# Three buffers for v and for raw weight words, with a new order of loads and new ranks, in a fused attention and mixture-of-experts kernel

## The chip, the cores and the metric

The kernel runs on one core of a Trainium2 chip. The metric is the device time of one execution in microseconds (us), the median of several runs. The engines are TensorE (PE for matmuls, PEld for its weight loads), VectorE (DVE), ScalarE (ACT), GpSimd (POOL) and SyncE (SP), which only issues DMA transfers.

## What is computed

Three layers follow each other. The first is Nyström attention over 4 batches, 8 heads, 576 tokens and 64 dimensions with 32 landmarks a head:

```python
A = sm(q, k_lm); Bm = sm(q_lm, k_lm); C = sm(q_lm, k)
Z = Bm.transpose(0, 1, 3, 2) / (norm1(Bm) * norminf(Bm) + 1e-06)
for _ in range(6):
    Z = 2 * Z - Z @ Bm @ Z
x = A @ Z @ C @ v
```

The second is a gated layer on the 2304 tokens of width 512: `h = x @ w_in` (512 x 2048), `g = h * clip(h + 3, 0, 6) / 6`, `x = g @ w_out` (2048 x 512). The third routes each token to one of 8 experts by `argmax(x @ w_gate)`, applies `relu(x @ w1) @ w2` of that expert up to a capacity, and scales by the token's gate probability. The weights w_in and w_out arrive as 64-bit words and have to be turned into 32-bit floats on the chip.

## The kernel before

The work falls into four stretches. In the first, q, k and v are loaded for 8 units (4 batches x 2 groups of 4 heads) and the attention of each unit is worked out: `turn_qk` forms landmark sums (on PE by `fold` matmuls into `ps_f`, L537, for units 0 to 3; on DVE by `sums`, L550, and one matmul, L554, for units 4 to 7), `landmark_scores` and `token_scores` form the scores (`pb`), `gather_v` multiplies the softmax with v (`ps_ct` L696, `ps_cl` L704, `pw` L715), `norms` (`ps_m` L670) and `newton` (`pn` L735, `px` L759) make the inverse. `project` multiplies the result with w_in (`ps_v` L362 into `vv`). In the second stretch `first` (`ph`, 6 matmuls each, L389) and `second` (`py`, 12 matmuls each, L433) run the gated layer for four quarters of the 2048 columns (`fq`) and 6 blocks of 288 tokens; `lasts` does the same for the last two blocks. The third stretch is the expert layer, unit by unit (`run_unit`: L1094, L1132, L1163, L1170). At the end a flag `redo` decides by a branch (`tc.If`, L1364) whether a general and slow path has to run over again; with these inputs it does not.

The order of the instructions in the first two stretches is made by a list scheduler in Python, the class `Order` (L39 to L107). Each job is a generator that yields steps (engine, estimated cost, buffers to take, events to wait for). `run` takes the step that can start first by its estimates, and among steps that can start at about the same time the one with the lowest rank; ranks come from the table `RANK`. `LOADS` is the order in which the loads of q and k (`qk`), v (`v`), w_in (`in`) and w_out (`out`) are issued; the loads of this list follow each other in that order on SP (`issue`). `BLOCKS` is the order of the blocks within each quarter. Each engine then runs its own instructions strictly in the order written, and waits for semaphores where a producer is late.

While the first `ph` has not been placed (`state["cold"]`), the scheduler puts filler matmuls on PE into the idle time that it expects: `keep_warm`, L983, one per 0.115 us beyond the first 0.3 us; they are the `warm` matmuls of L984 and compute nothing that is used.

Two buffer counts matter here. `convert` (L243) loads a 128 x 512 piece of 64-bit words into a tile `raw` (512 KB, L254), which is free again when ACT, DVE and, for the first quarter's pieces, POOL have made floats of it. `load_v` (L509) loads a unit's v into `vm` and `vl` (L515, L516), which are free again after the unit's `pw` matmuls. Both have two buffers, and the scheduler's table of slots has `raw=2` and `v=2`. The loads of the first expert's w1 (`w1_first`, L919) use `raw` too.

Of the kernel before, what the change touches and what calls it, by code (L numbers as in the profile page):

```python
# [8 lines left out]
F32 = mybir.dt.float32  # L9
# [3 lines left out]
U32 = mybir.dt.uint32  # L13
# [3 lines left out]
ET = mybir.EngineType  # L17
# [93 lines left out]

LOADS = [('qk', 1), ('in', 2), ('in', 1), ('qk', 0), ('v', 0), ('v', 1), ('in', 0), ('in', 3), ('qk', 2), ('v', 2), ('qk', 3), ('out', 1), ('out', 0), ('out', 2), ('qk', 4), ('v', 3), ('v', 4), ('out', 3), ('qk', 5), ('v', 5), ('qk', 7), ('v', 6), ('in', 6), ('in', 7), ('qk', 6), ('v', 7), ('in', 5), ('in', 4)]

RANK = {'w': -298.73, 'evict': 81.41, 'late': -13.54, 'fill': -244.58, 'logit': 110.18, 'route': -102.73, 'ahead': 67.77, 'unit2': 113.59, 'unit': 84.25, 'first2': 135.87, 'second2': 135.87, 'V2': -23.09, 'W': -6.44, 'u0': -30.37, 'u1': 44.61, 'u2': 38.52, 'u3': 45.53, 'u4': 84.73, 'u5': 65.31, 'u6': 98.5, 'u7': 118.66, 'cin0': 197.19, 'cin1': -0.9, 'cin2': 305.36, 'cin3': -23.6, 'cin4': 88.15, 'cin5': 450.88, 'cin6': 188.03, 'cin7': 280.69, 'cout0': -18.86, 'cout1': -66.49, 'cout2': 34.96, 'cout3': 65.88, 'V0': -74.78, 'V1': 84.97, 'V3': 134.52, 'V4': -441.95, 'V5': 37.92, 'V6': -57.56, 'V7': 31.31, 'out_1': 232.01, 'in_1': -9.42, 'wg_1': 188.44, 'out_2': 226.5, 'in_2': -334.43, 'wg_2': 114.87, 'out_3': -0.02, 'in_3': -179.05, 'wg_3': -27.51, 'C0': -161.31, 'C1': -15.08, 'C2': 6.94, 'C3': 1.79, 'C4': -17.7, 'C5': 55.68, 'C6': 42.33, 'C7': -71.74, 'A0': 130.29, 'A1': 103.73, 'A2': 144.67, 'A3': 116.13, 'A4': 122.48, 'A5': 121.43, 'A6': 133.45, 'A7': 202.82, 'B0': 44.41, 'B1': 144.53, 'B2': 64.17, 'B3': 62.65, 'B4': 51.27, 'B5': 35.89, 'B6': 91.91, 'B7': -6.21, 'Cv0': 42.94, 'Cv1': 52.0, 'Cv2': 35.34, 'Cv3': -62.91, 'Cv4': 45.36, 'Cv5': 17.68, 'Cv6': 36.1, 'Cv7': 38.02, 'Z0': -12.13, 'Z1': -62.3, 'Z2': -52.99, 'Z3': -37.97, 'Z4': -19.17, 'Z5': -52.94, 'Z6': -166.92, 'Z7': 12.86, 'sum0': 92.52, 'sum1': -22.5, 'sum2': 12.35, 'sum3': 52.44, 'sum4': 36.8, 'sum5': 57.28, 'sum6': -84.97, 'sum7': 33.35}

BY_PE = (0, 1, 2, 3)
BLOCKS = ((0, 0), (0, 1), (0, 2), (0, 3), (0, 4), (0, 5), (1, 0), (1, 3), (1, 2), (1, 1), (1, 4), (1, 5), (2, 0), (2, 2), (2, 3), (2, 5), (2, 1), (2, 4), (3, 2), (3, 0), (3, 1), (3, 3), (3, 4), (3, 5))
ROUTED = (0, 1, 3)  # L120
COMPACT = (2, 3, 4, 5, 6, 7)
G_BUFS, R_BUFS, QT_BUFS = 8, 2, 6


@with_exitstack
def nystrom_moe_kernel(ctx, tc, qt, kt, v, w_in, w_out, w_gate, w1, w2, capacity, out, dims, dbg=None):
    nc = tc.nc
    B, H, S, D = dims
    NT, DM = out.shape
    DFF = w_in.shape[1]  # L130
    E, _, F2 = w1.shape
# [3 lines left out]
    P = 128  # L135
# [3 lines left out]
    QW = DFF // NQ  # L139
# [880 lines left out]
    with tc.tile_pool(name="units", bufs=1, reuse_waits="tile") as up, \  # L1020
# [160 lines left out]
        def run_unit(i):  # L1181
# [11 lines left out]
            for t in range(NST):  # L1193
# [251 lines left out]
```

## Time and profile before

| what | value |
|---|---|
| median of 3 runs | 534.06 us (533.92 to 536.21) |
| the profiled execution's own time | 534.44 us |
| its span, first to last instruction | 532.7 us |
| PE busy | 518.9 us, 97% of the span |
| PEld busy | 452.3 us, 85% |
| DVE, ACT, POOL busy | 349.3, 293.9, 192.9 us (66%, 55%, 36%) |
| HBM read, written | 45.89 MB, 12.98 MB |

The profile shows one execution. The engines run beside each other, so their busy times overlap; PE is busy nearly all the time, though what it does in the first 50 us includes the filler matmuls, which count as busy. The time of an execution is a little more than its span (534.44 beside 532.7). The granted clock (PEclk) is the share of full speed that TensorE was allowed.

### The profile page before, as it was taken

How to read it: one execution, taken by the hardware profiler on the slowest of the kernel's cores; microseconds unless marked ns; L12 is line 12 of the kernel's file. 1: busy time of each engine (PE TensorE's matmuls, PEld its weight loads, DVE VectorE, ACT ScalarE, POOL GpSimd, SP SyncE). 2: the span in 40 equal slices, each digit the busy share in tenths (PEclk: the TensorE clock that was granted, in tenths of full speed). 3: DMA queues.
4: the chain of work that ended last, by engine and by line, in shares of the span. 5: the costliest groups of instructions: out<-in, count | busy, mean ns of one | idle time of the engine just before them, and what ended most of it. 6: DMA issues, size and time to landing. Idle time of an engine off the chain costs nothing. (4 is left out here: it accounts for less than half of the span.)

```text
span 532.7 us, 12062 instructions
## 1 busy us (share of the span) xinstructions
PE 518.9 (97%) x4781; PEld 452.3 (85%) x4781; DVE 349.3 (66%) x788; ACT 293.9 (55%) x684; POOL 192.9 (36%) x247
## 2 busy tenths in 40 slices
PE   8997999999999999999999999999999999999996
PEld 6664787968889998999998899998897899689784
DVE  1779867766479986675945555467735958987700
ACT  3776775966668554554545443444446564864411
POOL 3357967878434333311522112222160070016000
PEclk9999989999999999999999999999999999999999
DMA  7946741112352541214200020128921470510011
GB/s 292 312 178 222 270 151 49 38 46 75 89 184 93 189 143 51 76 40 135 80 1 1 1 90 2 41 93 281 323 96 41 172 281 0 175 53 23 2 50 44
DMA packets 24242, 59.74 MB, mean 112 GB/s; under 512 B 2928, under 2 KB 7536, under 8 KB 24176
## 3 DMA queue, kind: packets, MB, share of 16 engines
q1 hardware_dynamic: 23360, 58.60, 32.3%
q8 instruction: 39, 0.64, 0.5%
q10 hardware_dynamic: 816, 0.28, 0.2%
q14 instruction: 27, 0.22, 0.1%
HBM read 45.89 MB, written 12.98 MB: 111 GB/s over the span
## 5 line engine op out<-in xcount | busy, mean ns | idle before, releaser
L433 PE MATMUL py<-ghi,wo 128*128 128x288 f32 x768 | 159.1, 299 | 0.4 <-DVE yacc L445 0.4
L433 PEld LDWEIGHTS py<-ghi,wo 128*128 128x128 f32 x768 | 124.0, 190 | 5.1 <-issue 2.1
L389 PE MATMUL ph<-at,vv 128*128 128x288 f32 x768 | 120.8, 300 | 0.9 <-DVE st L662 0.8
L419 POOL TENSOR_TENSOR glo<-r,ghi 128x288 fp32r<-128x288 f32 x81 | 66.5, 830 | 150.4 <-ACT ghi L412 123.9
L433 PE MATMUL py<-glo,wo 128*128 128x288 f32 x384 | 113.9, 297 | 0.0
L389 PEld LDWEIGHTS ph<-at,vv 128*128 128x128 f32 x768 | 106.6, 188 | 8.6 <-issue 4.8
L400 ACT ACTIVATE r<-ph,half 128x288 f32<-128x288 f32 x128 | 63.6, 500 | 64.3 <-PE ph L389 54.2
L402 DVE SCALAR_TENSOR_TENSOR r<-r,ph 128x288 f32<-128x288 f32 x128 | 56.1, 447 | 29.0 <-ACT r L400 28.2
L433 PEld LDWEIGHTS py<-glo,wo 128*128 128x128 f32 x384 | 72.7, 189 | 0.0
L1163 PE MATMUL ps_o<-w2s,hT 128*128 128x512 f32 x288 | 66.2, 390 | 0.0
L1163 PEld LDWEIGHTS ps_o<-w2s,hT 128*128 128x128 f32 x288 | 53.8, 188 | 13.6 <-issue 2.4
L1053 POOL TENSOR_TENSOR w2s<-wi,w2s 128x512 fp32r<-128x512 f32 x24 | 31.5, 1353 | 88.1 <-ACT w2s L1052 88.1
L445 DVE TENSOR_TENSOR yacc<-py,yacc 128x288 f32<-128x288 f32 x72 | 32.5, 452 | 42.3 <-PE py L433 42.1
L412 ACT ACTIVATE ghi<-r 128x288 fp32r<-128x288 f32 x96 | 41.1, 441 | 23.1 <-DVE r L402 20.4
L1140 DVE TENSOR_TENSOR mix<-ps,mix 128x288 f32<-128x288 f32 x56 | 23.9, 451 | 11.6 <-PE ps L1132 11.0
L276 POOL TENSOR_TENSOR wo<-cvt,wo 128x512 fp32r<-128x512 f32 x16 | 21.9, 1368 | 22.7 <-ACT wo L274 22.6
L369 DVE TENSOR_TENSOR vv<-ps_v,vv 128x512 fp32r<-128x512 f32 x32 | 21.4, 683 | 11.4 <-ACT vv L367 11.3
L1079 ACT ACTIVATE hT<-mix 128x288 fp32r<-128x288 f32 x32 | 13.7, 443 | 26.8 <-DVE mix L1140 26.8
L735 PEld LDWEIGHTS pn<-yy 128*128 128x128 f32 x112 | 16.8, 189 | 9.4 <-issue 3.9
L735 PE MATMUL pn<-yy 128*128 128x96 f32 (+2 forms) x112 | 22.3, 294 | 0.8 <-POOL yy L687 0.5
L367 ACT ACTIVATE vv<-ps_v 128x512 fp32r<-128x512 f32 x32 | 18.2, 597 | 6.5 <-PE ps_v L362 6.3
L1174 ACT ACTIVATE rows_o<-ps_o,prob 128x512 f32<-128x512 f32 x12 | 8.3, 688 | 24.2 <-PE ps_o L1163 19.4
(219 smaller groups left out, 840.5 us busy)
## 6 DMA issues: line engine op xcount, KB each, us to landing
raw<-in_moe_w_in SPq DMA_DIRECT2D x16, 512.0 KB, 3.9
raw<-in_moe_w_out SPq DMA_DIRECT2D x16, 512.0 KB, 3.9
wi<-in_moe_w SPq DMA_DIRECT2D x6, 1024.0 KB, 6.6
r_d<-r SPq DMA_DIRECT2D x32, 144.0 KB, 1.8
vm<-in_v SPq DMA_DIRECT2D x8, 512.0 KB, 5.8
raw<-in_moe_w SPq DMA_DIRECT2D x4, 1024.0 KB, 5.9
qT<-in_q SPq DMA_DIRECT2D x6, 576.0 KB, 6.6
qT<-in_k SPq DMA_DIRECT2D x6, 576.0 KB, 7.7
```

What stands on the lines that cost most here:

```text
L276: nc.gpsimd.tensor_tensor(dst[1], xf, dst[0].bitcast(F32), op=ALU.subtract)
L389: nc.tensor.matmul(ph, lhsT=vv[pair][g][a][:, b, f * P:(f + 1) * P], rhs=at[pair][c][:, g, tok], start=n == 0, stop=n == 3 * NG - 1)
L400: nc.scalar.activation(r, ph, AF.Relu, bias=half, scale=1.0 / 6.0)
L402: nc.vector.scalar_tensor_tensor(r, r, 1.0, ph, op0=ALU.min, op1=ALU.mult)
L412: nc.scalar.activation(ghi, r, AF.Copy)
L419: nc.gpsimd.tensor_tensor(glo, r, ghi.bitcast(F32), op=ALU.subtract)
L433: nc.tensor.matmul(py, lhsT=w[a][:, f, d * P:(d + 1) * P], rhs=gh[f][c], start=f == 0 and n == 0, stop=f == NF - 1 and n == 2)
L445: nc.vector.tensor_tensor(y, py, y, op=ALU.add)
L735: nc.tensor.matmul(pn[:, cols], lhsT=yy[:, 0:P], rhs=yy[:, cols], start=True, stop=True)
L1053: engine.tensor_tensor(dst[1], src, dst[0].bitcast(F32), op=ALU.subtract)
L1140: plus = lambda dst, ps, x: nc.vector.tensor_tensor(dst, ps, x, op=ALU.add)
L1163: nc.tensor.matmul(ps, lhsT=hT[a][:, f, cols], rhs=w2s[c][:, f, :], start=n == 0, stop=n == 3 * FC - 1)
```

## The change

The tiles `vm`, `vl` and `raw` get three buffers, in the tile pools and in the scheduler's table of slots. `LOADS`, `BLOCKS` and nearly all numbers of `RANK` are replaced, so that the scheduler writes another order on every engine. A hint for the branch at the program's end is added for SP and ACT, and the scratch for dynamic DMA, which only the general path uses, is halved. From L1199 on, line numbers of the changed kernel are one higher.

```diff
-LOADS = [('qk', 1), ('in', 2), ('in', 1), ('qk', 0), ('v', 0), ('v', 1), ('in', 0), ('in', 3), ('qk', 2), ('v', 2), ('qk', 3), ('out', 1), ('out', 0), ('out', 2), ('qk', 4), ('v', 3), ('v', 4), ('out', 3), ('qk', 5), ('v', 5), ('qk', 7), ('v', 6), ('in', 6), ('in', 7), ('qk', 6), ('v', 7), ('in', 5), ('in', 4)]
+LOADS = [('qk', 1), ('qk', 0), ('in', 2), ('v', 0), ('in', 1), ('v', 1), ('in', 0), ('in', 3), ('qk', 2), ('v', 2), ('qk', 3), ('out', 0), ('v', 4), ('qk', 4), ('out', 3), ('out', 2), ('out', 1), ('v', 3), ('qk', 5), ('v', 7), ('in', 7), ('in', 6), ('v', 5), ('qk', 7), ('qk', 6), ('in', 4), ('in', 5), ('v', 6)]
...
-G_BUFS, R_BUFS, QT_BUFS = 8, 2, 6
+G_BUFS, R_BUFS, QT_BUFS, V_BUFS, RAW_BUFS = 8, 2, 6, 3, 3
...
-        raw = stage.tile([P, QW, 2], U32, tag="raw", name="raw")
+        raw = stage.tile([P, QW, 2], U32, tag="raw", name="raw", bufs=RAW_BUFS)
...
-    order = Order(dict(s=3, b=2, h=2, y=1, r3=2 * NF, g=2 * NF, r=R_BUFS, raw=2, cvt=2, part=1, qT=QT_BUFS, sums=2, lm=2,
-                       a1=2, a2=1, ec=2, eb=4, yy=4, rx=4, xx=2, ct=1, v=2))
+    order = Order(dict(s=3, b=2, h=2, y=1, r3=2 * NF, g=2 * NF, r=R_BUFS, raw=RAW_BUFS, cvt=2, part=1, qT=QT_BUFS, sums=2, lm=2,
+                       a1=2, a2=1, ec=2, eb=4, yy=4, rx=4, xx=2, ct=1, v=V_BUFS))
...
-        vm = late.tile([P, 4, 4 * D], F32, tag="vm", name="vm")
+        vm = late.tile([P, 4, 4 * D], F32, tag="vm", name="vm", bufs=V_BUFS)
...
-        c["vl"] = vl = late.tile([D, 4, D], F32, tag="vl", name="vl")
+        c["vl"] = vl = late.tile([D, 4, D], F32, tag="vl", name="vl", bufs=V_BUFS)
...
-        raw = stage.tile([P, F2], F32, tag="raw", name="raw_e")
+        raw = stage.tile([P, F2], F32, tag="raw", name="raw_e", bufs=RAW_BUFS)
...
+                    tc.mark_branch_hint_location("again", engines=(ET.SP, ET.Activation))
...
-            nest.enter_context(tc.If(again > 0))
+            nest.enter_context(tc.If(again > 0, label="again"))
...
-    nc = bacc.Bacc("TRN2", target_bir_lowering=False, num_devices=1, dynamic_dma_scratch_size=4096)
+    nc = bacc.Bacc("TRN2", target_bir_lowering=False, num_devices=1, dynamic_dma_scratch_size=2048)
```

How the order moves, at three places. First SP, the start of the program; `yacc_129` and `yacc_130` take q and k of unit 1, `yacc_127` and `yacc_128` those of unit 0 (a piece of the difference):

```order
+L1442 BRANCH_PREFETCH_HINT
 L506 DMA yacc_129<-in_q 128x1152
 L506 DMA yacc_130<-in_k 128x1152
-L254 DMA raw<-in_moe_w_in 128x1024 x2
 L506 DMA yacc_127<-in_q 128x1152
 L506 DMA yacc_128<-in_k 128x1152
-L515 DMA vm<-in_v 128x1024
-L516 DMA vl<-in_v 64x256
+L254 DMA raw<-in_moe_w_in 128x1024
+L515 DMA vm<-in_v 128x1024
+L516 DMA vl<-in_v 64x256
+L254 DMA raw<-in_moe_w_in 128x1024
```

Unit 0's q and k now stand right behind unit 1's; two pieces of w_in that stood ahead of them follow, with a v between them. The branch hint stands at the very start.

Second SP, from the loads of unit 3 to those of unit 4, with buffer numbers; before (`qT_432` and `qT_436` belong to unit 3, `qT_678` and `qT_683` to unit 4):

```order
L506 DMA qT_432<-in_q 128x1152
L506 DMA qT_436<-in_k 128x1152
L254 DMA raw_492<-in_moe_w_out 128x1024
L254 DMA raw_521<-in_moe_w_out 128x1024
L254 DMA raw_674<-in_moe_w_out 128x1024
L506 DMA qT_678<-in_q 128x1152
L506 DMA qT_683<-in_k 128x1152
L515 DMA vm_689<-in_v 128x1024
L516 DMA vl_690<-in_v 64x256
```

And now (`qT_417` and `qT_422` unit 3, `qT_486` and `qT_494` unit 4):

```order
L506 DMA qT_417<-in_q 128x1152
L506 DMA qT_422<-in_k 128x1152
L254 DMA raw_457<-in_moe_w_out 128x1024
L515 DMA vm_468<-in_v 128x1024
L516 DMA vl_469<-in_v 64x256
L506 DMA qT_486<-in_q 128x1152
L506 DMA qT_494<-in_k 128x1152
L254 DMA raw_521<-in_moe_w_out 128x1024
L254 DMA raw_584<-in_moe_w_out 128x1024
L254 DMA raw_671<-in_moe_w_out 128x1024
```

One piece of w_out instead of three stands ahead of unit 4's q and k; the other three have moved behind them.

Third PE, the stretch that leads to the first `ph`; before:

```order
L984 MATMUL warm<-ident 128x256
L578 MATMUL pb<-qT,lm 32x288 x8
L715 MATMUL pw<-vm,ct 32x64 x16
L715 MATMUL pw<-vl,ctl 32x64 x4
L670 MATMUL ps_m<-eb,mask_73 128x64
L696 MATMUL ps_ct<-ident,ec 128x128 x4
L735 MATMUL pn<-yy 128x96
L389 MATMUL ph<-at_117,vv_123 128x288
```

And now, where two fillers and the two rows of `pw` (L715) lie between the last row shown and the first `ph`:

```order
L984 MATMUL warm<-ident 128x256
L554 MATMUL ps_f<-sums,fold 128x256
L631 MATMUL pb<-lm 32x32 x4
L634 MATMUL pb<-qT,lm 32x288 x8
L704 MATMUL ps_cl<-ident,ec 64x128
L984 LDWEIGHTS ident
```

The landmark matmul L554 of a unit whose sums DVE makes now stands ahead of the first `ph`; it stood behind it. Over the whole program the matmuls are the same in kind and number but for the fillers, 109 before and 88 now. The first 44, ahead of the first `fold`, are unchanged. Behind them the groups were of 10, 15, 1, 11, 5, 1, 4 and 18 and are now of 8, 6, 3, 2, 3, 5, 2, 8, 5 and 2. On the other engines 7 of the subtractions that make `glo` have moved from DVE to POOL.

## Rows read from the trace of the kernel before

**Rows 1.** Windows between milestones: busy us (count) of each engine, clock, DMA.
```profile
core 0: us, PE busy (x) PEld busy (x) DVE busy (x) ACT busy (x) POOL busy (x), PEclk, DMA share, GB/s
0.00:9.05 9.05, 7.51 (x45) 5.57 (x45) 0.71 (x4) 1.28 (x1) 3.65 (x27) 1.00 0.67 236
9.05:49.45 40.40, 36.83 (x550) 24.91 (x549) 30.34 (x81) 31.02 (x84) 20.08 (x19) 1.00 0.71 250
49.45:68.92 19.47, 16.72 (x228) 12.95 (x227) 17.86 (x46) 13.74 (x40) 17.89 (x35) 0.99 0.83 277
...
80.00:150.00 70.00, 70.00 (x721) 58.47 (x721) 45.56 (x116) 48.82 (x126) 48.88 (x65) 1.00 0.20 61
150.00:350.00 200.00, 199.79 (x1957) 186.86 (x1959) 134.37 (x283) 104.47 (x229) 57.21 (x61) 1.00 0.24 75
350.00:400.00 50.00, 49.51 (x389) 46.05 (x382) 30.10 (x105) 22.74 (x58) 16.66 (x16) 1.00 0.58 204
...
527.43:532.70 5.27, 0.00 (x0) 0.00 (x0) 0.00 (x0) 0.69 (x1) 0.00 (x0) 0.99 0.15 56
```
**Rows 2.** Groups by line, PE, up to 49.4 us: the fillers.
```profile
L984 PE MATMUL warm<-ident 128*128 128x256 bf16 x109 | 16.0, 307 | 1.5 <-POOL ident L165 1.5
```
**Rows 3.** Timeline of PE: start, length, instruction, count.
```profile
1.54 7.57 PE L984 MATMUL warm<-ident 128*128 128x256 bf16 x44 [1.54 <-POOL ident L165]
...
13.14 1.81 PE L984 MATMUL warm<-ident 128*128 128x256 bf16 x15
14.88 2.19 PE L537 MATMUL ps_f<-yacc,fold 128*64 128x128 f32 x36
...
51.75 0.67 PE L554 MATMUL ps_f<-sums,fold 128*128 128x256 f32 x2 [1.16 <-DVE sums L550]
```
**Rows 4.** Waits of PE for one line: total, times, longest.
```profile
PE ps_m L670 <- DVE vv L369: 1.4, 1, 1.4
...
PE ps_m L670 <- ACT eb L667: 1.1, 1, 1.1
```
**Rows 5.** Timeline of SP's DMA issues: start, length over all of a row.
```profile
1.73 1.19 SPq L254 DMA_DIRECT2D raw<-in_moe_w_in  x2
2.96 0.53 SPq L506 DMA_DIRECT2D yacc<-in_q  x1
...
25.13 11.89 SPq L254 DMA_DIRECT2D raw<-in_moe_w_out  x3
37.07 0.42 SPq L506 DMA_DIRECT2D qT<-in_q  x1
```
**Rows 6.** Waits of SP's queue in the first 100 us: total, times, longest.
```profile
SPq L515 <- PE pw L715: 38.4, 5, 16.7
```
**Rows 7.** Windows of the start-up in which DMA rests or runs full.
```profile
32.00:37.00 5.00, 4.98 (x73) 3.63 (x77) 4.63 (x14) 4.74 (x12) 1.64 (x2) 1.00 0.01 2
...
8.00:16.00 8.00, 7.98 (x116) 6.32 (x115) 3.50 (x10) 4.89 (x12) 1.38 (x2) 1.00 1.05 379
```
**Rows 8.** The landmark sums on DVE: count, ns, first and last start.
```profile
L550 DVE TENSOR_REDUCE sums<-qT x8: 1310/1338/1347, 47.8 to 90.1; 128x128 f32<-128x1152 f32 x8
```
**Rows 9.** Windows of PE alone around the fall of its clock.
```profile
66.50:67.70 1.20, 0.43 (x2) 1.00 0.87 297
68.34:71.75 3.41, 3.41 (x17) 0.50 0.91 314
71.75:75.16 3.41, 3.41 (x141) 1.00 0.33 132
```
**Rows 10.** The end: sequencers of SP and ACT at the branch, SP's last wait.
```profile
L1364 SPq EVENT_SEMAPHORE  x2: 17/17/17, 530.4 to 530.5; - x2
L1364 ACTq EVENT_SEMAPHORE  x2: 17/17/17, 531.4 to 531.5; - x2
L1364 ACTq COMPARE_BRANCH  x1: 54/54/54, 528.6 to 528.6; - x1
...
L1441 SPq EVENT_SEMAPHORE  x2: 28/296/565, 530.9 to 531.0; - x2
```

More of the change, by code (lines that the diff above doesn't have):

```diff
@@ L110, in op @@
     return engine, cost, more, take, after, rank, port or engine == "POOL", tiles
-LOADS = [('qk', 1), ('in', 2), ('in', 1), ('qk', 0), ('v', 0), ('v', 1), ('in', 0), ('in', 3), ('qk', 2), ('v', 2), ('qk', 3), ('out', 1), ('out', 0), ('out', 2), ('qk', 4), ('v', 3), ('v', 4), ('out', 3), ('qk', 5), ('v', 5), ('qk', 7), ('v', 6), ('in', 6), ('in', 7), ('qk', 6), ('v', 7), ('in', 5), ('in', 4)]
-RANK = {'w': -298.73, 'evict': 81.41, 'late': -13.54, 'fill': -244.58, 'logit': 110.18, 'route': -102.73, 'ahead': 67.77, 'unit2': 113.59, 'unit': 84.25, 'first2': 135.87, 'second2': 135.87, 'V2': -23.09, 'W': -6.44, 'u0': -30.37, 'u1': 44.61, 'u2': 38.52, 'u3': 45.53, 'u4': 84.73, 'u5': 65.31, 'u6': 98.5, 'u7': 118.66, 'cin0': 197.19, 'cin1': -0.9, 'cin2': 305.36, 'cin3': -23.6, 'cin4': 88.15, 'cin5': 450.88, 'cin6': 188.03, 'cin7': 280.69, 'cout0': -18.86, 'cout1': -66.49, 'cout2': 34.96, 'cout3': 65.88, 'V0': -74.78, 'V1': 84.97, 'V3': 134.52, 'V4': -441.95, 'V5': 37.92, 'V6': -57.56, 'V7': 31.31, 'out_1': 232.01, 'in_1': -9.42, 'wg_1': 188.44, 'out_2': 226.5, 'in_2': -334.43, 'wg_2': 114.87, 'out_3': -0.02, 'in_3': -179.05, 'wg_3': -27.51, 'C0': -161.31, 'C1': -15.08, 'C2': 6.94, 'C3': 1.79, 'C4': -17.7, 'C5': 55.68, 'C6': 42.33, 'C7': -71.74, 'A0': 130.29, 'A1': 103.73, 'A2': 144.67, 'A3': 116.13, 'A4': 122.48, 'A5': 121.43, 'A6': 133.45, 'A7': 202.82, 'B0': 44.41, 'B1': 144.53, 'B2': 64.17, 'B3': 62.65, 'B4': 51.27, 'B5': 35.89, 'B6': 91.91, 'B7': -6.21, 'Cv0': 42.94, 'Cv1': 52.0, 'Cv2': 35.34, 'Cv3': -62.91, 'Cv4': 45.36, 'Cv5': 17.68, 'Cv6': 36.1, 'Cv7': 38.02, 'Z0': -12.13, 'Z1': -62.3, 'Z2': -52.99, 'Z3': -37.97, 'Z4': -19.17, 'Z5': -52.94, 'Z6': -166.92, 'Z7': 12.86, 'sum0': 92.52, 'sum1': -22.5, 'sum2': 12.35, 'sum3': 52.44, 'sum4': 36.8, 'sum5': 57.28, 'sum6': -84.97, 'sum7': 33.35}
@@ new lines @@
+LOADS = [('qk', 1), ('qk', 0), ('in', 2), ('v', 0), ('in', 1), ('v', 1), ('in', 0), ('in', 3), ('qk', 2), ('v', 2), ('qk', 3), ('out', 0), ('v', 4), ('qk', 4), ('out', 3), ('out', 2), ('out', 1), ('v', 3), ('qk', 5), ('v', 7), ('in', 7), ('in', 6), ('v', 5), ('qk', 7), ('qk', 6), ('in', 4), ('in', 5), ('v', 6)]
+RANK = {'w': -324.32, 'evict': 83.82, 'late': -40.82, 'fill': -283.19, 'logit': 115.24, 'route': -67.75, 'ahead': 60.78, 'unit2': 228.82, 'unit': 172.63, 'first2': 135.87, 'second2': 135.87, 'V2': -1.6, 'W': 21.51, 'u0': -28.47, 'u1': 32.79, 'u2': 35.49, 'u3': 62.85, 'u4': 87.03, 'u5': 67.21, 'u6': 98.05, 'u7': 86.73, 'cin0': 197.35, 'cin1': -50.99, 'cin2': 248.78, 'cin3': -9.35, 'cin4': 135.9, 'cin5': 345.74, 'cin6': 310.9, 'cin7': 262.93, 'cout0': -13.21, 'cout1': -99.85, 'cout2': 19.88, 'cout3': 36.18, 'V0': 23.49, 'V1': 55.15, 'V3': 116.61, 'V4': -414.62, 'V5': -35.95, 'V6': -28.65, 'V7': 45.4, 'out_1': 248.01, 'in_1': 5.82, 'wg_1': 193.53, 'out_2': 216.47, 'in_2': -357.88, 'wg_2': 93.91, 'out_3': 60.21, 'in_3': -184.63, 'wg_3': 59.03, 'C0': -103.59, 'C1': -118.17, 'C2': 36.44, 'C3': 25.37, 'C4': -16.9, 'C5': 27.97, 'C6': -221.84, 'C7': -161.11, 'A0': 130.07, 'A1': 167.92, 'A2': 142.99, 'A3': 94.12, 'A4': 94.97, 'A5': 157.79, 'A6': 177.77, 'A7': 224.0, 'B0': 51.77, 'B1': 182.22, 'B2': -8.69, 'B3': 54.03, 'B4': 50.48, 'B5': 27.58, 'B6': 50.93, 'B7': 39.36, 'Cv0': -41.75, 'Cv1': 91.73, 'Cv2': 57.74, 'Cv3': -90.81, 'Cv4': 45.22, 'Cv5': -1.59, 'Cv6': 11.17, 'Cv7': 29.45, 'Z0': -1.29, 'Z1': -202.01, 'Z2': -66.69, 'Z3': -54.4, 'Z4': -18.34, 'Z5': 6.19, 'Z6': -82.66, 'Z7': 20.14, 'sum0': 83.12, 'sum1': -67.6, 'sum2': 18.63, 'sum3': 31.82, 'sum4': 29.7, 'sum5': 59.53, 'sum6': -169.43, 'sum7': 26.04}
@@ L118 @@
 BY_PE = (0, 1, 2, 3)
-BLOCKS = ((0, 0), (0, 1), (0, 2), (0, 3), (0, 4), (0, 5), (1, 0), (1, 3), (1, 2), (1, 1), (1, 4), (1, 5), (2, 0), (2, 2), (2, 3), (2, 5), (2, 1), (2, 4), (3, 2), (3, 0), (3, 1), (3, 3), (3, 4), (3, 5))
+BLOCKS = ((0, 0), (0, 1), (0, 2), (0, 3), (0, 4), (0, 5), (1, 1), (1, 5), (1, 0), (1, 3), (1, 4), (1, 2), (2, 4), (2, 5), (2, 1), (2, 3), (2, 0), (2, 2), (3, 4), (3, 0), (3, 1), (3, 2), (3, 3), (3, 5))
 ROUTED = (0, 1, 3)
 COMPACT = (2, 3, 4, 5, 6, 7)
-G_BUFS, R_BUFS, QT_BUFS = 8, 2, 6
+G_BUFS, R_BUFS, QT_BUFS, V_BUFS, RAW_BUFS = 8, 2, 6, 3, 3
```

## The prediction

> **What bounds the kernel now.** I read the windows first [rows 1]. From 80 to 150 us PE is busy 70.00 of 70.00 us, from 150 to 350 us 199.79 of 200.00, from 350 to 400 us 49.51 of 50.00: there PE's own work is the time, and a better order can win back the 0.70 us of idle and no more. The rest of what PE loses lies in the start-up and at the end. Behind the first `fold`, at 9.05 us, PE is idle 40.40 - 36.83 = 3.57 us up to the first `ph` at 49.45 and 19.47 - 16.72 = 2.75 us up to the first `py` at 68.92. Idle time is only half of the story, because fillers count as busy: all 109 take 16.0 us [rows 2], of which the first 44 take 7.57 [rows 3], and these wait for the first q and k, which no order brings sooner. The other 65 take 16.0 - 7.57 = 8.43 us, 0.130 us each. So the pot that the change can draw on in the start-up is 8.43 + 3.57 + 2.75 = 14.75 us.
>
> What fills the pot is seen on SP. Unit 0's q is issued behind two pieces of w_in [rows 5], and PE passes 1.81 us with 15 fillers before unit 0's `fold` [rows 3]. Later three pieces of w_out take SP 11.89 us to issue, from 25.13 to 37.02, since the third waits for one of two `raw` tiles, and unit 4's q is issued only at 37.07 [rows 5]. DMA, which moves 379 GB/s when it has work, lies at 2 GB/s from 32 to 37 us [rows 7]. For a free v tile SP waited 38.4 us in five waits [rows 6]. A late unit 4 makes a late `sums`: DVE starts the first of them at 47.8 [rows 8], and PE waits 1.16 us for them before L554 at 51.75 [rows 3].
>
> At the end the last output is on its way while ACT's branch, at 528.6, needs until 531.4 to go on. SP has seen its own transfers in at 530.4 to 530.5, comes to its wait at 531.0 and stands there 0.565 us, for ACT [rows 10].
>
> **The change part by part.** The matmuls are the same but for 21 fillers, so the sum goes by what PE no longer waits.
>
> (a) Fillers: 21 fewer by 0.130 us are 2.7 us. The scheduler wrote them for waits that it expected, so a filler that goes saves its time only if the wait behind it goes too: the ends are 0 and -2.7. I stand near the full end, because the 15 fillers that go as one group have a plain cause that goes with them. Two pieces of 512 KB no longer stand ahead of unit 0's q and k; at 379 GB/s [rows 7] they take 1.05 MB / 379 GB/s = 2.8 us, more than the 1.81 us that PE filled. I take -2.2.
>
> (b) The idle 3.57 us up to the first `ph`: 1.4 and 1.1 us of it are two waits of `ps_m`, for a DVE and an ACT instruction ahead of it in those engines' order [rows 4]. Both engines were busy three quarters of that stretch (30.34 and 31.02 of 40.40 us [rows 1]) and get the same work in another order. Nothing in the trace says which way these waits go: I take 0, with ends of -1.4 and +1.4, the longer wait gone or doubled.
>
> (c) The idle 2.75 us up to the first `py`: unit 4's loads now stand ahead of three of the four w_out pieces, so the wait of 1.16 us on `sums` need not come there. L554 now stands ahead of the first `ph`, though, where a late sum holds up all that follows. DVE is busy 17.86 of 19.47 us here and POOL 17.89 [rows 1], so what is freed may be stopped by them. I take half, -0.6; the ends are -2.75 and +1.2, the wait doubled.
>
> [...] At half speed 3.41 us of PE's time do 1.7 us of work, so this fall costs 1.7 us. A hole of the same size in the new order would bring it again, none would save it, one more would cost as much: 0, with ends of -1.7 and +1.7.
>
> (e) The hint: if ACT's 2.8 us at the branch go, SP finds ACT done and the end comes up to 0.565 us sooner; SP's own wait for the transfers still stands. No row shows a hint; it can save 0 to 0.57. I take -0.45, near the full wait, because ACT would have 531.0 - 528.6 = 2.4 us to spare. [...]
>
> (f) From 70 us to the end of PE's work: the same matmuls in another order. The 0.70 us of idle may go or double, so 0 with ends of -0.7 and +0.7. The third `raw` lets w1 pieces come sooner, which PE did not wait for. Moving 7 subtractions to POOL costs nothing, since POOL is busy 48.88 of 70.00 us up to 150 us and 57.21 of 200.00 after that [rows 1]. The halved scratch belongs to the path that is not run.
>
> The sum is -2.2 + 0 - 0.6 + 0 - 0.45 + 0 = -3.25 us. Against the profiled execution's own 534.44 us that is 531.2; that execution stands 0.38 us above the median of 534.06, from which it would be 530.8. I forecast **531.0 us**. About 0.5%, here 2.7 us, is what a measurement of this kernel can tell from no change, so the forecast lies just beyond it.
>
> **The rivals.**
>
> The waits stay (A). The start-up is a chain of small steps over DVE, ACT and POOL, and the fillers only marked the place where PE waited for it. Then 21 fillers become 2.7 us of idle and the end alone is gained. For it: DVE and POOL are nearly full from 49 to 69 us [rows 1]. Against it: unit 0's chain waits for a load that comes 2.8 us sooner. Time: 534.06 - 0.45 = 533.6 us.
>
> More goes than fillers (B). With DMA no longer resting from 32 to 37 us, DVE has its sums earlier, the hole before 67.70 closes and the clock does not fall: -3.25 and -1.7 from (d), 529.1 us. For it: one hole alone brought the fall. Against it: PE is busy a smaller part of a stretch without its fillers. [...]
>
> A new wait ahead of the first `ph` (C), the slower side. L554 stands in PE's order before the first `ph`, so all `ph` now wait for unit 4's sums. If DVE, with the rest of its work unchanged, comes to them no sooner than 47.8, L554 starts at 51.75 and takes 0.67: the first `ph` comes at 52.4 at the earliest, not at 49.45, 3.0 us later, less the 1.16 us that are no longer waited later: +1.8. No filler saves anything then, and PE stands for some us, which brings the clock down once more: +1.7. With the end's -0.45 it is 534.06 + 3.05 = 537.1 us. It decides at a start of the first sum of about 45 us: two of 1.338 us and L554 then end at 48.4, and what stands between L554 and the first `ph` puts that at its old place. For it: DVE takes 30.34 of 40.40 us. Against it: DVE is idle 10 us of that stretch, and unit 4's q no longer waits for 37.07.
>
> The hint does nothing (D): inside the forecast's range, 0.45 us above it.
>
> **How the numbers follow.** I give the forecast, with D in it, 0.50, A 0.22, B 0.18 and C 0.10. The forecast's own range is 529.6 to 532.6 us: it holds one of the ends of (b), 1.4 us, either way. The range that should hold 8 in 10 reaches over B and A: 528.4 to 535.0. Its low end is B with an end of (f), its high end A with the end of (b); C, and the rare case in which all the ends meet, are left out. Faster by over 0.5% means below 531.4 us: seven tenths of the forecast's 0.50, 0.35, and nearly all of B, 0.17, together 0.52. Within 0.5%: the rest of the forecast, all of A and the little of B and C that falls there, 0.39. Slower: 0.09, C.
>
> **What would show it.** In the profile after, the fillers' group should have 88 instructions and some 13.3 us, the first `ph` should start at 46 to 48 us and the first `py` at about 66 us. SP should issue unit 4's q before 30 us, and DMA should not rest from 32 to 37 us. ACT's event behind the branch should follow within half a us. If the first `ph` comes at 49 us or later, (a) was wrong. If L554 is in PE's waits with over 2 us, it is C. If the clock is granted below 1.00 more than once behind 10 us, or not at all, (d) was wrong. A time above 535.0 us would say that I overlooked a wait.

## The result, and the profile after

The changed kernel takes 529.06 us (median of 5 runs, 528.60 to 529.99) beside 534.06 (533.85 to 536.21, 5 runs in the same comparison): a ratio of 0.9909, 95% interval 0.9891 to 0.9927. The profiled execution took 529.06 us with a span of 527.3, beside 534.44 and 532.7: 5.4 us less in the span.

PE in windows between the same milestones as in [rows 1] (start of the first `fold`, the first `ph`, the first `py`, the third layer's first matmul, the end of PE's work), of the changed kernel; columns as there:

```profile
9.23:46.78 37.55, 34.42 (x522) 22.10 (x521) 28.46 (x77) 28.14 (x78) 20.46 (x31) 1.00 0.90 326
46.78:63.50 16.72, 14.78 (x194) 11.99 (x188) 16.06 (x48) 14.27 (x44) 15.34 (x19) 1.00 0.74 248
...
63.50:374.81 311.31, 310.24 (x3143) 281.62 (x3141) 204.42 (x472) 177.33 (x411) 129.68 (x154) 1.00 0.25 83
374.81:522.67 147.86, 147.84 (x869) 127.85 (x868) 93.35 (x183) 72.18 (x151) 31.58 (x24) 1.00 0.28 102
...
522.67:527.25 4.58, 0.00 (x0) 0.00 (x0) 0.00 (x0) 0.69 (x1) 0.00 (x0) 0.87 0.17 63
```

The first `ph` comes 2.67 us sooner than before, the first `py` 5.42. PE's idle up to the first `ph` is 37.55 - 34.42 = 3.13 us (it was 3.57), up to the first `py` 1.94 (2.75), behind it up to the third layer 1.07 (0.70), at the end 4.58 (5.29). From the first `fold` to PE's last matmul the clock stays at 1.00 in every row; the fall of [rows 9], to 0.50, isn't there, and the 0.87 of the last row lies behind PE's work.

The fillers and PE's waits up to 70 us, from the groups by line and the list of waits, beside [rows 2, 4]:

```profile
L984 PE MATMUL warm<-ident 128*128 128x256 bf16 x88 | 14.2, 318 | 1.5 <-POOL ident L165 1.5
```
```profile
PE pn L735 <- POOL yy L687: 1.5, 1, 1.5
PE ps_cl L704 <- ACT ct L700: 0.9, 1, 0.9
PE ps_f L554 <- DVE sums L550: 0.5, 1, 0.5
```

Both waits of `ps_m` in [rows 4] are gone (one of 0.5 us for POOL has come), and the one for `sums` has halved, though L554 now stands ahead of the first `ph`. The longest wait, 1.5 us of `pn`, is new and lies behind the first `ph`, ahead of 56.63 us. PE's timeline at the start, and SP's issues, beside [rows 3, 5]:

```profile
1.55 7.75 PE L984 MATMUL warm<-ident 128*128 128x256 bf16 x44 [1.55 <-POOL ident L165]
...
43.26 0.67 PE L554 MATMUL ps_f<-sums,fold 128*128 128x256 f32 x2 [0.49 <-DVE sums L550]
```
```profile
1.84 0.43 SPq L506 DMA_DIRECT2D yacc<-in_q  x1
...
26.70 0.33 SPq L506 DMA_DIRECT2D qT<-in_q  x1
28.06 0.33 SPq L506 DMA_DIRECT2D qT<-in_k  x1
28.48 8.87 SPq L254 DMA_DIRECT2D raw<-in_moe_w_out  x3
```

Unit 0's q is issued 1.12 us sooner and unit 4's 10.4 us sooner, ahead of the w_out pieces on which SP stands. From 32 to 37 us DMA now moves 389 GB/s where it moved 2 [rows 7]:

```profile
32.00:37.00 5.00, 4.87 (x64) 2.88 (x65) 4.13 (x13) 3.69 (x10) 3.08 (x4) 1.00 1.02 389
```

The first sum starts at 37.6 in place of 47.8 [rows 8], and SP stands 9.4 us behind `pw` in place of 38.4 [rows 6]; its longest waits in the first 100 us are now for `raw` tiles, 33.1 us behind DVE's L236 and 24.4 behind POOL's L268.

**The clock, which one profile doesn't show.** The fall of [rows 9] comes in some executions of a kernel and not in others. Of 68 runs of the kernel before in the comparisons below, 18 had a mean clock of 0.999 or more, with a median of 532.98 us, and 43 had 0.997 or less, with 534.23. Of 11 runs of the changed kernel 5 lie at 0.999 or more, median 528.88, and 5 at 0.996, median 530.04. So runs at the lower clock take either kernel about 1.2 us longer, and between runs at the same clock the change is worth 4.1 to 4.2 us. The profiled span's 5.4 also holds a fall that only the execution profiled before had.

### The profile page after: what moved, and what is told of

Read it like the earlier page. It is cut to its first block, busy times and chain, and to the rows that moved or that the text cites. A ratio compares the mean times of both kernels' runs of the same rounds, so it can differ in the third digit from the quotient of the medians.

```text
span 527.3 us, 12038 instructions
## 1 busy us (share of the span) xinstructions
PE 515.0 (98%) x4760; PEld 449.2 (85%) x4760; DVE 343.0 (65%) x781; ACT 293.9 (56%) x684; POOL 200.7 (38%) x254
## 5 line engine op out<-in xcount | busy, mean ns | idle before, releaser
L419 POOL TENSOR_TENSOR glo<-r,ghi 128x288 fp32r<-128x288 f32 x88 | 74.5, 849 | 137.7 <-ACT ghi L412 80.3
```

Source lines behind the costliest of these rows:

```text
L419: nc.gpsimd.tensor_tensor(glo, r, ghi.bitcast(F32), op=ALU.subtract)
```

## The experiments

Each ran beside the kernel before on the same chip, whose median there was 533.6 to 534.0.

### The buffers alone, and the new tables without them

The kernel before with a third physical buffer; the scheduler's slots, and so the order of all engines, as they were:

```diff
-        raw = stage.tile([P, QW, 2], U32, tag="raw", name="raw")
+        raw = stage.tile([P, QW, 2], U32, tag="raw", name="raw", bufs=3)
...
-        vm = late.tile([P, 4, 4 * D], F32, tag="vm", name="vm")
+        vm = late.tile([P, 4, 4 * D], F32, tag="vm", name="vm", bufs=3)
```

(`raw_e` and `vl` likewise, and the scratch halved.)

> The kernel before, every instruction in its old order, with three tiles for raw, vm and vl instead of two (and the halved scratch that makes room). Theory 1 (the new order of loads is what counts; buffers only serve it): the 65 fillers stay on PE, so only waits on SP go: sums start sooner than 47.8 us, the 1.16 us wait for them goes, the fall of the clock behind 66.5 us may go (1.7 us): 531.5 to 533.5 us. Theory 2 (the buffers alone carry it, the order is their by-product): SP issues unit 4's q at about 30 instead of 37 us and the time is that of the changed kernel, 529 to 530 us. Theory 3 (nothing but PE's order counts): 534 us.

Measured: 533.51 us (531.87 to 535.04, 12 runs), ratio 0.9995 (0.9978 to 1.0012). SP's issues:

```profile
22.54 4.27 SPq L254 DMA_DIRECT2D raw<-in_moe_w_out  x3
26.86 0.42 SPq L506 DMA_DIRECT2D qT<-in_q  x1
```

Unit 4's q goes out at 26.86, as early as in the changed kernel, and nothing is gained by it, as theory 3 had it: DVE comes to the first sum at 47.20 us, without a wait for the load. The order of PE and DVE asks for it no sooner. PE's waits are those of before:

```profile
PE ps_m L670 <- DVE vv L369: 1.4, 1, 1.4
PE ps_f L554 <- DVE sums L550: 1.1, 1, 1.1
PE ps_m L670 <- ACT eb L667: 1.1, 1, 1.1
```

Its execution ran at full clock (mean 1.000), over the same hole ahead of the first `py`: in the 4 us up to there PE was busy 2.65 us in it, as in the kernel before. That makes it the fair partner for the profile after. The first `fold` starts 0.92 us sooner in it than in the changed kernel's, for a reason that the last section gives. These are its windows:

```profile
8.31:48.81 40.50, 36.83 (x550) 24.91 (x549) 30.25 (x81) 30.55 (x84) 20.09 (x19) 1.00 0.88 315
48.81:68.01 19.20, 16.46 (x228) 12.68 (x227) 17.63 (x44) 13.61 (x40) 17.60 (x35) 1.00 0.68 232
68.01:378.44 310.43, 308.97 (x3099) 279.69 (x3097) 207.38 (x480) 175.40 (x409) 120.06 (x143) 1.00 0.26 84
526.08:531.38 5.30, 0.00 (x1) 0.00 (x0) 0.00 (x0) 0.69 (x1) 0.00 (x0) 0.97 0.15 56
```

The other way round, the changed kernel with two of each, laid out anew by the scheduler with the new tables:

```diff
-G_BUFS, R_BUFS, QT_BUFS, V_BUFS, RAW_BUFS = 8, 2, 6, 3, 3
+G_BUFS, R_BUFS, QT_BUFS, V_BUFS, RAW_BUFS = 8, 2, 6, 2, 2
```

> The changed kernel with V_BUFS and RAW_BUFS set to 2: loads, ranks and blocks stay new, the scheduler lays the order out again for two buffers and puts 94 fillers on PE instead of 88. Theory 1: 6 fillers are 0.8 us, and SP waits again for raw and v tiles in front of unit 4's q: 530 to 531.5 us. Theory 2: most of the gain goes, 533 to 534 us. If the buffers play no part: 529.1 us.

Measured: 542.48 us (541.02 to 543.79, 5 runs), ratio 1.0151 (1.0127 to 1.0175). A miss for both theories. Its first `ph` comes at 44.74 us, sooner than the changed kernel's, but its first `py` only at 73.39, 9.9 us later. With two buffers for v alone (`V_BUFS` 2, `RAW_BUFS` 3):

> The changed kernel with two buffers for v and three for raw words, ordered by the scheduler with the new ranks and loads; 88 fillers, as in the changed kernel. With two of both the time was 542.5. Theory 1 (v's third buffer is what the new ranks live on: SP stood 38.4 us behind pw matmuls before and 9.4 after): most of the 13.4 us come back, 538 to 543. Theory 2 (the raw buffer is): the time stays at 529 to 531, and most of the loss goes with raw.

Measured: 563.16 us (561.76 to 563.54, 5 runs), ratio 1.0547 (1.0520 to 1.0575), worse than with two of both and again a miss for both theories. Its first `py` starts at 64.89, near the changed kernel's; the loss comes later. From 186 to 206 us PE is busy 5.39 of 20 us and waits for w_out pieces. SP issues these late: the order has put them behind a transfer of zeros into the output (L800), for which SP stands 31.2 us until POOL has made the zeros:

```profile
SPq L800 <- POOL logit L794: 31.2, 1, 31.2
...
SPq L515 <- PE pw L715: 29.5, 6, 9.5
```
```profile
PE py L433 <- ACT wo L274: 11.1, 2, 8.0
```

The chain from SP's wait to PE's isn't followed step by step here. So these two runs don't weigh a buffer. A slot count changes what the scheduler writes, and the tables fit the one count that they were made for. The new order with fewer physical buffers wasn't tried, so which of the two third buffers it needs is open.

### One load moved, all other orders held

Unit 0's q and k: the changed kernel with its first loads in the order of before (v of unit 0 follows them); PE, DVE, ACT and POOL keep their instructions to the last row.

```diff
+held = []
...
-        nc.sync.dma_start(raw.rearrange("p n t -> p (n t)"), src.bitcast(U32))
+        nc.sync.dma_start(raw.rearrange("p n t -> p (n t)"), src.bitcast(U32)); [nc.sync.dma_start(*h) for h in held if (out, fq, n) == (False, 0, 1)]
...
-        nc.sync.dma_start(qT, (qt, kt)[i][n])
+        held.append((qT, (qt, kt)[i][n])) if n == 0 else nc.sync.dma_start(qT, (qt, kt)[i][n])
...
```

(Unit 0's v is held in the same way.)

> The changed kernel with the first loads in the order of the kernel before: two w_in loads issued ahead of unit 0's q and k; every other engine's order, the fillers too, is as in the changed kernel. Theory 1 (unit 0's early load is what brings the first ph forward): q and k of unit 0 land about 2.5 us later (two loads of 1.27 us), k at about 14.4 in place of 11.9; the second fold, which started at 13.32, starts at 14.4 to 14.6, and everything behind it on PE comes 1.1 to 1.3 us later: first ph at about 47.9, time 530.2 (529.9 to 530.5). Theory 2 (the start is set by something later, as the wait on vv or eb that the kernel before has between 42 and 49 us): first ph stays within 0.3 us of 46.78 and the time at 529.1.

Measured: 530.70 us (529.57 to 530.95, 6 runs), ratio 0.9939 (0.9916 to 0.9961): 1.2 to 1.6 us above the changed kernel's two medians. PE does wait for k at the second `fold`:

```profile
PE ps_f L537 <- DMA yacc<-in_k: 1.1, 1, 1.1
```

Its first `ph` came at 46.91, only 0.13 later; in this execution the first `fold` had started at 8.35, 0.88 sooner than in the changed kernel's, so the two differ by 1.0 us counted from there. Its clock fell later, ahead of the first `py` (0.61 granted from 56 to 59 us, 0.82 from 59 to 62), and 4 of 6 runs had 0.996. Between runs at the same clock the load is worth 0.7 to 0.8 us: the run at 0.999 took 529.57 beside 528.88, the four at 0.996 a median of 530.85 beside 530.04. Theory 1 has the sign and the mechanism, at about two thirds of the size in time.

The mirror image, the kernel before with unit 0's q and k first and without the 15 fillers:

```diff
+held = []
...
-        nc.sync.dma_start(raw.rearrange("p n t -> p (n t)"), src.bitcast(U32))
+        (lambda *h: held.append(h) if (out, fq) == (False, 0) and n in (1, 2) else nc.sync.dma_start(*h))(raw.rearrange("p n t -> p (n t)"), src.bitcast(U32))
...
-        nc.sync.dma_start(qT, (qt, kt)[i][n])
+        nc.sync.dma_start(qT, (qt, kt)[i][n]); [nc.sync.dma_start(*h) for h in held if (n, i) == (0, 1)]
...
-            for _ in range(int(max(0.0, idle - 0.3) / 0.115)):
+            for _ in range((lambda m: m if m != 15 else 0)(int(max(0.0, idle - 0.3) / 0.115))):
```

> The kernel before with unit 0's q and k issued ahead of the two w_in loads, and without the group of 15 fillers (1.8 us) that stands ahead of unit 0's fold; else its orders. Theory 1 (this load and these fillers are worth what the prediction's first term says): the second fold starts at about 13.2 in place of 14.88, first ph 1.4 to 1.8 us sooner, time 1.4 to 1.8 us less than before: 532.0 to 532.4 beside 533.8. Theory 2 (behind it the kernel before waits anyway, 1.37 us on DVE's vv and 1.06 us on ACT's eb, for work that unit 0 does not set): first ph within 0.4 us of 49.1, time 533.8.

Measured: 535.15 us (534.42 to 536.26, 12 runs), ratio 1.0026 (1.0010 to 1.0042): slower, which neither theory had. ACT's timeline says why:

```profile
12.52 0.66 ACT L230 ACTIVATE wi<-raw 128x512 f32<-128x512 f32 x1 [7.63 <-DMA raw<-in_moe_w_in]
13.21 0.67 ACT L262 ACTIVATE raw<-raw 128x512 f32<-128x512 f32 x1
13.78 1.10 ACT L543 ACTIVATE lm<-ps_f 64x128 f32<-64x128 f32 x4
```
```profile
14.94 0.23 PE L631 MATMUL pb<-lm 64*32 64x32 f32 x4 [2.75 <-ACT lm L543]
```

The old ranks put the conversion of w_in ahead of `lm` on ACT. Its load now comes behind unit 0's, so ACT starts the conversion at 12.52 us in place of 9.20, and PE waits 2.75 us for `lm` (it started these matmuls at 12.45 before). In the changed kernel `lm` is ahead of that conversion in ACT's queue, so the w_in loads can be late:

```profile
11.46 1.12 ACT L543 ACTIVATE lm<-ps_f 64x128 f32<-64x128 f32 x4 [6.56 <-PE ps_f L537]
...
14.29 0.67 ACT L230 ACTIVATE wi<-raw 128x512 f32<-128x512 f32 x1
```

Unit 4's q and k: the changed kernel with these two behind the w_out pieces, as `held` above but with `n == 4` and let go at `(out, fq, n) == (True, 0, 1)`.

> The changed kernel with unit 4's q and k issued behind the fourth w_out load, which waits for a raw buffer until 37 us, in place of at 26.7 and 28.1; all other orders as in the changed kernel. Theory 1 (the order of the changed kernel has unit 4's landmark sums ahead of the first ph, and can afford it only because the third buffer lets that load go early): q and k land at about 42 and 43.5 in place of 35.6 and 37.1, the first sum on DVE, in its order at 37.64, starts 4 us later and holds DVE's queue, first ph comes at 50 to 51, time 532 to 534. Theory 2 (the load could as well be late, other work covers it): first ph within 0.5 us of 46.78, time 529.1.

Measured: 534.02 us (533.54 to 536.12, 12 runs), ratio 1.0008 (0.9994 to 1.0023): the whole gain is gone. SP issues unit 4's q at 37.00 us, as late as in the kernel before. DVE and PE wait, and then the clock falls (windows of PE alone: busy, clock, DMA share, GB/s):

```profile
DVE sums L550 <- DMA qT<-in_q: 4.5, 1, 4.5
```
```profile
PE px L759 <- DVE xx L753: 4.5, 1, 4.5
```
```profile
38.90:43.50 4.60, 0.11 (x2) 0.89 0.99 354
43.50:48.40 4.90, 4.90 (x32) 0.50 0.88 286
```

PE doesn't wait for the sums themselves but for an instruction of a Newton step that stands behind them in DVE's queue. The first `ph` comes at 51.85, 5.07 us later; counted from the first `fold` (8.10 here, 9.23 there) it is 6.2 us: 4.5 of wait, and 1.7 that I put down to the 4.90 us at 0.50, an estimate. All 12 runs had a mean clock of 0.990 to 0.993. This is rival C, made by hand: it lies in wait in the new order, and the early load keeps it off.

### Fillers and hint

Without any filler (`if False and state["cold"]:` in `keep_warm`):

> The changed kernel without its 88 filler matmuls, all else in the same order; what is left out computes nothing that is used. [...] If fillers cost their own time (44 behind the first fold, 0.13 us each): as much as 5.7 us less, 523.5 to 527 us.

Measured: 534.95 us (530.34 to 537.60, 12 runs), ratio 1.0008 (0.9979 to 1.0037). The two runs at 0.999 took 530.34 and 530.65, the nine at 0.997 or less a median of 535.42. So even at full clock nothing is won when all of them go, since PE waits in their place: from 9.23 us to its first `ph` at 47.79 it is idle 8.0 of 38.6 us. And the mean clock is lower: the nine runs go down to 0.983, where none of the kernel before lies under 0.994. The first `fold` also ran slowly:

```profile
8.87 3.65 PE L537 MATMUL ps_f<-yacc,fold 128*64 128x128 f32 x34 [0.71 <-DMA yacc<-in_k]
...
14.41 2.19 PE L537 MATMUL ps_f<-yacc,fold 128*64 128x128 f32 x36
```

The last section comes back to this pace.

Without the hint (the `mark_branch_hint_location` line and the label removed):

> The changed kernel without the hint for the branch. If the hint is worth what SP waited for ACT in the kernel before: ACT's event comes some 2.8 us behind its branch again instead of 0.5, and the time is 0.5 to 0.65 us longer, 529.6 to 529.7 us. If ACT's wait at the branch was hidden: 529.1 us.

Measured: 529.38 us (528.63 to 529.93, 6 runs), ratio 0.9911 (0.9892 to 0.9930), 0.3 us above the changed kernel, which lies inside both intervals: inconclusive in time. The branch and the event behind it on ACT, without the hint and then with it:

```profile
L1364 ACTq EVENT_SEMAPHORE  x2: 17/17/17, 526.9 to 527.0; - x2
...
L1364 ACTq COMPARE_BRANCH  x1: 54/54/54, 524.1 to 524.1; - x1
```
```profile
L1365 ACTq EVENT_SEMAPHORE  x2: 17/17/17, 524.4 to 524.4; - x2
...
L1365 ACTq COMPARE_BRANCH  x1: 68/68/68, 523.9 to 523.9; - x1
```

ACT's stall of 2.8 us has become 0.5. SP's events behind the branch (count, then shortest, median and longest in ns) show its wait of 0.565 us for ACT, and that it is gone with the hint:

```profile
L1441 SPq EVENT_SEMAPHORE  x14: 17/28/565, 526.1 to 528.1; - x14
```
```profile
L1442 SPq EVENT_SEMAPHORE  x14: 17/28/28, 525.6 to 527.2; - x14
```

From the end of PE's work to the end of the span it is 5.29 us without and 4.58 with the hint. All ten profiled executions with a hint take 4.58 to 4.91 us there, all four without one 5.29 or 5.30.

With the hint on ACT alone (`engines=(ET.Activation,)`), beside the changed kernel once more:

> The changed kernel itself, unaltered, on the chip and in the rounds of the next two runs, so that they have something to be compared with: 529.1, 528.6 to 530.0; runs at a mean clock of 0.999 near 528.8 and runs at 0.996 near 529.9.

> The changed kernel with the branch hint on ACT alone and none on SP. In the kernels with a hint on both, the first load is issued 0.1 us later (0.93 beside 0.82) and lands at 6.8 to 7.4 us; in those without, at 6.5 to 6.7. Theory 1 (the hint on SP delays the first loads and so gives back at the start a part of what ACT's hint saves at the end): the first load is issued at 0.82, lands at 6.5 to 6.8, first ph comes 0.3 to 0.7 us sooner; SP's event behind the branch at the end comes later by about 0.4 us, as without a hint; the time is 528.8 to 529.1. Theory 2 (where the first load lands differs from run to run, and the hint has no part in it): landing and first ph stay within what the changed kernel shows, and the time is 0.4 us longer for SP's end: 529.3 to 529.6.

Measured: the changed kernel 529.54 us (528.60 to 530.77, 6 runs), ratio 0.9916 (0.9893 to 0.9939); the hint on ACT alone 529.17 (528.28 to 529.76, 6 runs), 0.9906 (0.9885 to 0.9928). The first load goes out at 0.82 and lands at 6.80, not 0.93 and 7.32; the first `ph` comes at 46.04, not 46.66; the end takes 4.74 us, not 4.77. So the load does land sooner, but it isn't what brings the first `ph` forward: the first `fold` stands behind the 44 fillers and starts when they end, at 8.50 and 9.19 us, and from there to the first `ph` it is 37.5 us in both. The fillers took 7.02 and 7.72 us, for the reason in the last section. The 0.4 us between the medians lies inside both intervals: inconclusive in time.

### The old `BLOCKS`, and three edits together

The changed kernel with the old `BLOCKS`:

> The changed kernel with the table BLOCKS of the kernel before (the order in which the second layer's blocks are worked through); the first 947 rows of PE's queue are the same. Theory 1 (the gain is made before the first py, and BLOCKS has no part in it): 529.1, within 0.5 us of the changed kernel on the same chip. Theory 2 (the new BLOCKS keep PE fed behind it, where the old ones would wait for r and ghi): 530 to 532, with PE idle by 1 to 3 us between the first py and the third layer, where it is 1.07 us now.

Measured: 528.37 us (528.04 to 528.61, 5 runs), ratio 0.9889 (0.9866 to 0.9911). All 5 runs had a clock of 0.999 or more; against runs of the changed kernel at that clock (528.88) it is 0.5 us less. The windows behind the first `py` agree, the changed kernel run beside it first:

```profile
63.37:374.62 311.25, 310.18 (x3144) 281.58 (x3142) 204.22 (x472) 176.81 (x410) 129.50 (x154) 1.00 0.25 83
```
```profile
63.28:374.07 310.79, 309.71 (x3143) 281.51 (x3142) 207.42 (x482) 175.24 (x411) 121.54 (x145) 1.00 0.26 85
```

The idle time is the same, 1.07 and 1.08 us; the matmuls follow each other 0.47 us closer. So the new `BLOCKS` have no part in the gain and probably cost half a us; the intervals of the medians overlap. The work that moved from DVE to POOL came with them: DVE is busy 207.42 again.

Last, the old `BLOCKS`, the hint on ACT alone, and 38 fillers in place of the first 44:

```diff
-            for _ in range(int(max(0.0, idle - 0.3) / 0.115)):
+            for _ in range((lambda m: {44: 38}.get(m, m))(int(max(0.0, idle - 0.3) / 0.115))):
```

> The changed kernel with the old BLOCKS (528.37 by itself), the hint on ACT alone, and 38 in place of 44 fillers at the start. Those 44 took 6.4 to 7.75 us in the profiles of kernels with the same start, and the first fold began when they ended (7.87 to 9.23), though unit 1's q was there at 6.7 to 7.4. Theory 1 (in executions where they end late, the fillers hold the first fold back): the first fold starts at 7.4 to 8.5, first ph comes at 45.4 to 46.2 in place of 46.7, the time is 0.5 to 1.0 us less than with the old BLOCKS alone: 527.4 to 527.9. Theory 2 (the chain behind is set by k and by ACT's lm, or fewer fillers bring the clock down): 528.3 or more.

Measured: 529.77 us (527.62 to 531.09, 6 runs), ratio 0.9932 (0.9910 to 0.9954). The one run at full clock is the fastest of all, 527.62, with the first `fold` at 8.40 and the first `ph` at 45.98, as theory 1 had it; the other five had 0.994 to 0.997 and took 529.15 to 531.09. Theory 2 holds in the median. Whether the six fillers or another of the three edits brings the clock down more often, or chance does, isn't told apart. The old `BLOCKS` alone have the lowest median.

## Why the prediction was right, and where it wasn't

The range (528.4 to 535.0) held 529.06, and the sign was right. The forecast of 531.0 was 1.9 us too high, and 529.06 lies below the forecast's own range of 529.6 to 532.6. The time is that of rival B, 529.1, but not for B's reason, so that it hits B's figure is luck. Term by term, against the profile before and against the fair partner (the order of before at full clock):

| term | predicted | profile before to after | fair partner to after |
|---|---|---|---|
| (a) fillers, total | -2.2 | 16.0 to 14.2: -1.8 | 15.3 to 14.2: -1.1 |
| (b) idle up to the first `ph` | 0 | 3.57 to 3.13: -0.4 | 3.67 to 3.13: -0.5 |
| (c) idle up to the first `py` | -0.6 | 2.75 to 1.94: -0.8 | 2.74 to 1.94: -0.8 |
| (d) clock, and PE's work without fillers | 0 | 502.9 to 500.8: -2.1 | 501.4 to 500.8: -0.6 |
| (e) the end | -0.45 | 5.29 to 4.58: -0.7 | 5.30 to 4.58: -0.7 |
| (f) idle behind the first `py` | 0 | 0.70 to 1.07: +0.4 | 1.46 to 1.07: -0.4 |
| sum | -3.25 | -5.4 | -4.1 |

PE's work without fillers is its busy time of the page less the fillers' row: 518.9 - 16.0, 516.7 - 15.3, 515.0 - 14.2.

Counted from the first `fold`, the fair partner took 523.07 us and the changed kernel 518.02, 5.05 less: the start, which the first 44 fillers set, went 0.92 us against the changed kernel in this pair.

**The step that failed is (d), the term on the clock.** It read the fall of [rows 9], 3.41 us at a granted clock of 0.50 (1.7 us of work lost, by estimate) behind a stretch in which PE was busy 0.43 of 1.20 us, as one that the order decides: "A hole of the same size in the new order would bring it again". With three buffers the order of before ran over the same hole and on at full clock (2.65 of 4.00 us busy up to 68 us, 7.00 of 7.00 from there to 75, both at 1.00). And the new order has a hole as long, the 1.5 us of `pn` ahead of 56.63: in the changed kernel's profile the clock stays up behind it, in the profile without the hint it falls behind the same hole (PE alone; the changed kernel first):

```profile
55.10:56.63 1.53, 0.01 (x1) 1.00 0.78 260
56.63:60.00 3.37, 3.37 (x36) 1.00 0.87 299
```
```profile
54.00:55.53 1.53, 0.00 (x1) 1.00 0.76 182
55.68:59.09 3.41, 3.41 (x25) 0.50 0.94 337
```

So such a hole brings a fall in some executions and not in others, and the sum was made against a profile that had one. Between the two executions of the old order it is worth 502.9 - 501.4 = 1.5 us of PE's work (the term's ends had 1.7), of which 0.76 come back, since PE idles 0.70 us behind the first `py` in place of 1.46. The term should have read: this execution has a fall that others may not have, so make the sum against a run without it. What decides in which executions the clock falls stays open.

Of the 1.9 us by which the forecast was too high, about one is terms that were too small (4.1 at equal clock beside 3.25) and the choice between 531.2 and 530.8. The rest is where the two medians lie, 534.06 near the runs of the kernel before at a lower clock (534.23), 529.06 near the runs of the changed kernel at full clock (528.88). With 43 of 68 and 5 of 11 runs at the lower clock that is in part luck. B's words "the clock does not fall" came true in this profile, but B's cause, a hole that closes, isn't what the runs show. And the 1.00 of the first row of [rows 1] doesn't mean full pace through the start-up: up to about 7 us PE took a filler every 0.213 us, behind that one every 0.109, as the last section shows.

(a) was right in kind and its price fits where it was worked out: the fillers behind the first 44 went from 8.43 to 14.2 - 7.75 = 6.45 us, -2.0. The first 44, which I took as the same in both, took 7.57, 6.83 and 7.75 us in these three executions. Nor do they only wait for the first q and k: before, these had landed at 6.49 and 7.90 us, and the first `fold` started at 9.05, when the fillers ended. The cause that I gave is half of it. Later loads of unit 0 cost the changed kernel 1.2 to 1.6 us in the median (0.7 to 0.8 at equal clock); but earlier loads alone, with the old ranks, cost the kernel before 1.15 us. "A plain cause that goes with them" is a load and the place of `lm` in ACT's queue, together.

(b) stayed within its ends: both waits of `ps_m` went, and one of 0.9 us and some of half a us came. (c) was right within 0.2 us, though by another sum than its own: the wait for `sums` and the smaller ones behind it went, and the 1.5 us of `pn` came. What stood under it, unit 4's early load, is worth more than its term: without it the changed kernel takes 534.02. Rival C named this, and its point of decision (a first sum by 45 us) was met with 37.6.

(e) was right, as far as the profiles tell (in time, 0.3 us, it is inconclusive): the ten executions with a hint end 0.4 to 0.7 us sooner than the four without one, and the 0.7 of this profile is the upper end. The wait that it names went, from 565 to 28 ns. The rest is when the last output lands, 2.0 to 2.3 us behind its issue in these executions. The hint on SP gave nothing that shows there: with ACT's alone the end takes 4.74 and 4.60 us. ACT's event follows its branch by 0.5 us with the hint and by 2.8 without it, so the hint does something there; by what means, no run shows. Rival D falls with that.

Rival A, 533.6, falls for the change as a whole. For each part alone it holds, or the time is longer still: the buffers alone 533.51, the new order with unit 4's load late 534.02, unit 0's load early in the old order 535.15. The gain is in having them together; the new ranks alone, with all old loads, were not run. On the clock: with 88 fillers for 109, runs at a mean of 0.997 or less are no more frequent here (5 of 11, 43 of 68 before); with none, the mean clock goes down to 0.983.

## What to carry to other kernels

A list of loads, the ranks and the buffer counts of such a scheduler are one object: each edit tried by itself was worth nothing or cost time, because an engine that keeps its order turned the saved wait into another (ACT behind w_in, for which PE waited 2.75 us; DVE behind unit 4's q, 4.5 us); ask of every load moved back which queue meets its consumer first. Before costing a clock fall from one profile, look at the clocks of several runs, and compare runs at the same clock. Keep part of a change that shows no gain of its own under suspicion: the new `BLOCKS` rode along at a price of about half a us.

## What was not expected of the hardware

The same 44 filler matmuls took 7.57 us in the kernel before, 7.75 in the changed kernel, 7.02 with the hint on ACT alone and 6.39 without the hint; the windows' rows of the first two show a granted clock of 1.00 there. But the traces' records of the granted clock begin only at 6.90, 7.27, 5.76 and 4.48 us, and a window counts time without a record as 1.00. In the traces of before and after, the fillers ahead of the first record follow each other every 0.213 us, those behind it every 0.109. In the changed kernel (fillers alone):

```profile
3.00:7.00 4.00, 4.00 (x21) 1.00 0.81 281
7.30:9.20 1.90, 1.90 (x18) 1.00 1.01 401
```

So PE starts at half its later pace, though no record gives the clock of that stretch, and in these four executions the later the first record, the longer the 44 fillers and the later the first `fold` (4.48, 5.76, 6.90 and 7.27 us for the record; 6.39, 7.02, 7.57 and 7.75 for the fillers; 7.87, 8.50, 9.05 and 9.23 for the `fold`). The changed kernel run again has 7.19 us beside 7.27, the edits of it with the same first instructions on PE 4.48 to 6.98; what sets it isn't shown. Without fillers PE's first matmul came at 7.50 us and the first record at 11.92, and 34 matmuls of `fold` took 3.65 us where 36 take 2.19. A run's mean clock doesn't hold this start, which differs by up to 1.4 us between these executions.

And the branch hint isn't free: issued by SP at 0.8 us, it moved the first load from 0.82 to 0.93 us, and that load landed at 7.1 to 7.4 us in the executions with the new order of loads and this hint, at 6.7 to 6.8 in those with the same order and no hint on SP. Where the fillers stood ahead of the first `fold`, this cost nothing that the traces show, since the `fold` began when they ended.
